# A new order of all groups in a planned attention-and-mixer kernel on one core

## The chip, the core and the metric

The kernel runs on one core of a Trainium2 chip. Its engines are TensorE (PE, matmuls; PEld is its weight load), VectorE (DVE), ScalarE (ACT), GpSimd (POOL) and SyncE (SP, which only issues DMAs here). The metric is device time in microseconds (us), less is better. The time before is the median of 13 runs.

## What is computed

A gated linear recurrence over 768 steps (4 batches, 8 heads of 48), and on its output a low-rank mixing over the sequence and a two-layer network over the channels. Inputs and output are float32.

```python
def _attn_ref(q, k, v, alpha):              # all (4, 8, 768, 48)
    for t in range(S):
        state = alpha[:, :, t, :, None] * state + einsum('bhd,bhe->bhde', k[:, :, t], v[:, :, t])
        y[:, :, t] = einsum('bhd,bhde->bhe', q[:, :, t], state)

def _moe_ref(x, U, V, w_ch1, w_ch2):        # x: y as (4, 768, 384); U (768, 32), V (32, 768)
    h = x.transpose(0, 2, 1) @ U @ V
    u = x + h.transpose(0, 2, 1)
    return u + np.maximum(u @ w_ch1, 0.0) @ w_ch2    # 384 -> 1536 -> 384
```

## The kernel before

**Tiling.** The recurrence is worked in units of 128 rows, six to a batch. In batches 0 and 1 a unit is a half of the heads over 256 steps, each partition holding two neighbouring steps (`stage_pair`); in batches 2 and 3 it is all heads over 128 steps (`stage_gla`). "Unit 1.3" is the unit 3 of batch 1. A unit goes through these groups of instructions:

- four loads by SP (alpha, k, q, v) into one of 36 `io` slots;
- ACT takes the logarithm of alpha, PE adds it up by matmuls with triangular masks (the decay sums, L461 to L470 or L685 to L687), ACT forms the exponentials `ai` and `aa` and the decay of the whole unit;
- DVE or POOL scales k and q by them (`rk`, `rq`; L492 or L722), PE transposes both (L507 or L743), ACT or DVE copies the transposed tiles out of PSUM (`kt`, `qt`);
- PE forms the scores (L531 or L759) into two PSUM banks, DVE masks them (`pm`, L542 or L769);
- PE forms the unit's contribution to the state (L570 or L782). In batch 0 a matmul with the identity (L560) adds the state so far on PE, and DVE multiplies the sum by the decay (`st`); elsewhere DVE adds (`sm`), and DVE or POOL multiplies;
- PE forms the output from masked scores and v (`rv`, a bf16 copy) and from q and the state (L617 and L629, or L851 and L849), ACT or DVE copies it to `xb`.

In batch 3 all transpositions of k and q go by DMA instead: ACT issues two `DMA_TRANSPOSE` for each unit (L732 to L736), twelve in all.

`stage_mix` then makes the low-rank sums (L869), the mixed rows and their transposition `uT` (L888 and L891 in batch 0; L903, DVE additions, and L926 elsewhere). `mlp1` makes the hidden layer: 24 groups to a batch, each three matmuls of 384 columns (L953) and a ReLU by ACT or DVE (L963, L965). `mlp2` makes each of six output row blocks in groups of four matmuls (L983), DVE adds the residual (L995), SP stores. The weights come as 24 loads, each copied to bf16 by POOL, ACT or DVE. Mode tags of the groups (F, Q, R, C, V) say how a group tiles the PE array: whole, in quarters, in halves of the rows, in strips of the columns, or in strips of the rows.

**The order.** Every group is handed to a planner with `P.add`, which names the engines that can do it, a cost for each and what it reads and writes; `add` numbers the groups, 0 to 1061. `TABLE` is one list of all the numbers, and the groups are emitted in its order: each engine works off its own groups of that list, in that order, and waits for what they read. A letter behind a number picks the engine (V for DVE, A for ACT, G for POOL); without one the first engine named is taken. `place` walks the list with the planner's own costs, and from that comes two things only: which slot of a ring (PSUM bank, `io` slot and so on) a buffer gets, and how many matmuls on a zero tile ("fillers", L331) go into PE's expected gaps before 28 us. For a DMA that ACT issues it assumes this landing:

```python
if op.mode == "X":
    clock[eng] = t + cost
    end[op] = t + (5000.0 if dma > t + 800.0 else 3800.0) - self.LAT[eng]
    dma = max(dma, t) + 300.0
```

The numbers that the next sections use:

| group | number |
|---|---|
| loads of alpha of 0.1 and 0.4, of q of 0.1 | 71, 83, 73 |
| decay sums of units 0.2, 0.0, 0.1, 0.3, 0.4 | 211, 165, 188, 236, 261 |
| unit 0.0: scaled k; copies of the transposed k and q; scores; masks; contribution and state; identity matmul | 169; 173, 174; 175; 176, 177; 178, 179; 180 |
| unit 0.2: copies of k and q; scores; masks; identity matmuls | 219, 220; 221; 222, 223; 225, 227 |
| unit 0.1: state, identity matmul | 202, 203 |
| hidden-layer groups of batch 0: the first of the old table, the first of the new one; another, with the last of its weight loads and the copy of that | 340, 328; 358, 25, 26 |
| unit 1.0: transposition of k, its copy, scores | 418, 420, 422 |
| unit 1.3: decay sums, scaling of q, its transposition | 483, 488, 490 |
| transposes by ACT: units 3.0 to 3.5 | 871, 872; 888, 889; 906, 907; 924, 925; 942, 943; 959, 960 (k first) |
| scores of units 3.1, 3.4, 3.5 | 890, 944, 961 |
| unit 3.2's scaling of q, its load | 905, 149 |
| ReLUs of batch 0; a ReLU of batch 2 (of hidden-layer group 795); a weight copy of the second layer | 341, 349, 361, 371; 796; 48 |

Of the kernel before, what the change touches and what calls it, by code (L numbers as in the profile page):

```python
# [156 lines left out]


TABLE = """
75 2 3 4 5 209 211 67 76 163 165 79 234 214 167 69 77 68 170V 212 215G 236 217 172 238 213 216V 166 169V 218 171 174V 220V 173V 175 176 83 70 81 237  # L160
168 219A 71 78 164G 80 178 221 179 223 73 72 87 74 0 241G 180 222 181 84 186 259 239 188 210G 240G 190 189 261 224 225 226 177 264 263 192V 1 193G 187G
242 227 243 244A 262 245V 229 230 231 194 246 232V 282 191 196A 233V 228 247 248 182 195 284 197A 184A 201 198 183 85 287 285 265G 82 88 202 266V 267
203 269A 235G 89 268 199 204 200 86 270A 185A 286 249 250 251 271 90 91 7 288G 254 289V 8 260G 95 6 33 99 252 256 35 31 23 39 10 290 258A 253 272 273
292A 19 41 21 37 27 25 107 29 291 255 205 274 275 293A 276 294 257A 295 296 283A 277 57 297 298 279 206 9G 410 34G 32G 412 278 299 208A 207V 300 301
302 304V 101 92 100 47 96 97 94 415 280A 281A 303A 13 16 305 306 93 43 55 45 49 14A 311 308 314 317 307A 51 63 59 53 456 315 309 433 98 103 312 17V
313A 458 318 320 310V 323 321 324 322V 325V 435 11 20V 319V 36A 316A 340 338 342 362 339V 61 436 461 438 341A 366 22G 42G 364 24A 460 363A 12A 38V 40V
365V 352 328 437 367A 414 30A 459 65 102 111 108 104 109 105 329V 343V 26V 28V 463V 106 462G 326 348 349A 506 413 330 368 354 360 355V 331V 336 508
353V 416V 439V 112 346 332 511 347A 369A 333A 372 373V 334 335V 337V 327V 440G 358 356 465 344 464 467V 510 361A 509 359A 442 411G 417G 115 113 444V
345A 357A 466A 418 441 350 419 425 443V 420V 421V 351A 46A 48A 468 15 44G 56G 50G 110 114 426 469 445 422 370 116 424 423 446 470 371A 52A 380 386 54G
64G 429 430 432V 447 58A 431A 434A 374 375 448 452 62G 427 428V 449 60V 66V 450 387 381 453 454A 117 481 483 376 457V 455V 476 471 477 382 486 485 529  # L170
484 531 377 472 512G 514 388 473V 487V 513V 474 516V 515 392 489 488V 451G 383 532 533 517A 491V 479V 389 482G 490 478 492A 480A 535G 534 653 393 496
497 493 518 498G 536G 495 494 119 394 655 537 398 538 379 378 123 390 127 399 499 520 395 519 475G 500G 530G 507A 539A 656 659V 501 521 544 540A 658
657 541 660G 503 661 545 400 502 662A 505A 522 504A 663 542 543 524 547 523G 546V 664V 526 672 549 551A 548 525 550A 674 118 391 124 121 120 129 131
528V 135 133 122 125 527V 665 552 404 676 677 553A 675 692 712 554 654G 401 666 137 139 667 132 126 564 559 555 560 556 561 405 406 557 670 562 668 565
566 694 714 567 563V 669 558A 587 585 589 696 716 695 715 717 590A 732 671V 679V 568V 573 609 605 407 610V 698G 579 615 606V 616V 571 580A 586A 588A
752 591 734 592A 697 700 577 678V 572V 701V 754 673G 719G 699G 756 737 755 680 607 134 613 608V 578V 595 575 682 687 574V 681V 688 614V 611 576A 736
612A 596A 603 702 581 601 703V 689G 597 569 599 604A 582A 735 598A 570A 863 600A 602A 683V 128 385 136 384 408 758G 739G 693G 738G 704 684 705 685 686
583 707 617 740 722 584A 708 723V 718G 865 618 690 867 130 141 403 706 159 151 147 138 757G 709V 691V 866 741A 713G 619 710 761 762A 720 742 593 759
760A 594A 721V 629 620 143 409 146 396 621 622 402 868 727 743V 630 728 140 148 145 155 724 744 898 952 916 753A 733G 18 870G 729G 763 711V 765 726 764
635 636 745 725 746 631 623 747 637 900 901 624 730 750 748 749V 766 767V 632 880 731A 882 902 751A 883 903 885 884 872 625 869G 638 626 768 628 871  # L180
641 642 152 153 627 149 397 142 769V 780 775 776 770 777 771 781 782 643 918 919 772 887G 904G 647 954 648 778 783 649 773 889 920 779V 784V 144 634
150 811 922G 923G 934 956 955 812A 921 924 774V 829 813 873 787 830V 814V 160 874 799 800V 875 650 819 793 815 794V 644 816V 936 809 827 825 810V 823
791 828V 785 905G 881G 864G 886G 899G 788A 925 907 876 906 888 957G 824V 826V 786V 877 797 803 893 821 878 157 792A 798A 938 894 804V 156 154 161 805
806V 801 158 941V 802V 937 879A 939 822A 820A 817 926 890 908 940G 818A 928 959 789 790A 892 891 909 917G 895G 958G 853 910 795 796V 943 942 807 808V
896 831 911 912 833 854 935G 960 914 947 929 927 913V 930 931V 948 949V 915A 832A 858 834 835 859 633 162 855 953V 836 837 944 946 961 945 860 838 839
950 932 652 963 962 646 964 651 645 856 843 840 861 951V 933A 965A 897A 966 848 967A 841 978 968 973 980 975 974 979 844 849 970 969 845 976 977A 857
842 862 981 850 971 982V 1015 1016V 1025 1007 1011 1013 1027 972V 991 1008V 993 994A 1028A 1026A 851 846 1009 995 1001 999 1023 1002A 1014A 1024A 992A
1021 1019 1029 1022V 1012V 1017 1010A 1020A 1018A 983 1046 1047 1030V 1048 1049 984A 989 990V 987 1051 1005 1003 1004V 639 1050 985 1052 997 1053 986V
988V 1054 640 1055 852 996A 1031 1041 1036 998V 1042 1006A 1000A 1043 1044 1032 1037 1038 1033 1056 1045 847 1039 1040 1034 1057 1059 1060 1035 1058
1061  # L190
"""

# [6 lines left out]
def kernel(  # L199
# [12 lines left out]
    nc = tc.nc  # L212
    B, H, S, D = q.shape
    C = 128
    NC = S // C
    HP = H // 2
    DM = H * D
# [23 lines left out]
    P = Plan()  # L241
# [16 lines left out]
    for x in (filler, tri, ident, mask2, blocks):  # L258
        nc.vector.memset(x, 0.0)  # L259
    nc.gpsimd.affine_select(  # L260
        out=tri, in_=tri, compare_op=ALU.is_gt, fill=1.0, base=0, pattern=[[1, 2], [-1, C]], channel_multiplier=1
# [3 lines left out]
        out=mask2, in_=mask2, compare_op=ALU.is_gt, fill=1.0, base=0, pattern=[[1, 2], [-1, 2], [-2, C]], channel_multiplier=2  # L265
# [703 lines left out]
    def mlp2(b, xb, ub, utx, h1, c):  # L969
        tt = c // NT  # L970
        low = b in XT
        base = xb if low else ub
        ou = Buf(outs)
        parts = [(0, 256), (256, DM)] if b == B - 1 and c == NC - 1 else [(0, DM)]
        for n, (lo, hi) in enumerate(parts):
            hb = Buf(bank)
            groups = [range(NJ)] if len(parts) > 1 else [range(4 * g, 4 * g + 4) for g in range(3)]
            for g, jts in enumerate(groups):
                last = jts[-1] == NJ - 1

                def f(e, jts=jts, hb=hb, lo=lo, hi=hi, last=last):
                    for jt in jts:
                        nc.tensor.matmul(  # L983
                            hb()[:, 0 : hi - lo], lhsT=h1()[:, jt, c * C : (c + 1) * C], rhs=w2_sb[:, jt, lo:hi],
                            start=(jt == 0), stop=(jt == NJ - 1 and not low),
                        )
                    if low and last:
                        nc.tensor.matmul(hb()[:, 0 : hi - lo], lhsT=vp_sb[:, c * C : (c + 1) * C], rhs=utx()[:, lo:hi], start=False, stop=True)

                need = [(h1, tt, jt) for jt in jts] + [("w2", jt) for jt in jts] + ([utx] if low and last else [])  # L990
                cost = mm(*[hi - lo] * (len(jts) + (1 if low and last else 0)))
                P.add({"PE": cost}, f, r=need, w=[hb])

            def f_o(e, hb=hb, lo=lo, hi=hi):
                nc.vector.tensor_tensor(ou()[:, lo:hi], base()[:, c, lo:hi], hb()[:, 0 : hi - lo], op=ALU.add)  # L995

            P.add({"DVE": 70 + 398 * (hi - lo) // DM}, f_o, r=[hb] + (xk(b, xb, c) if low else [(ub, c)]), w=[(ou, n)])

            if b not in PAIR:
                P.add(  # L1000
                    {"SP": 550.0 * (hi - lo) / DM + (0 if len(parts) == 1 else 60)},
                    lambda e, lo=lo, hi=hi: nc.sync.dma_start(out[b, c * C : (c + 1) * C, lo:hi], ou()[:, lo:hi]),
                    r=[(ou, n)],
                )
                continue
            for z in range(2):

                def f_store(e, z=z):
                    nc.sync.dma_start(out[b, c * C : (c + 1) * C, :].rearrange("(m j) x -> j m x", j=2)[z], ou()[64 * z : 64 * z + 64, :])

                P.add({"SP": 300.0}, f_store, r=[(ou, n)])

    small()
    weights1()
# [49 lines left out]
```

## Time and profile before

| | |
|---|---|
| median of 13 runs | 163.08 us (161.56 to 164.98) |
| the profiled execution | 161.81 us, its span 160.0 us |
| PE idle before its first matmul | 1.19 us |
| fillers on PE | 16 |
| DMA, bytes moved | 30.39 MB, mean 190 GB/s |
| transposes by ACT: issue to landing, least, median, most | 3.4, 4.5, 6.1 us |
| ACT held by one such issue | 1.21 to 1.67 us |

The span goes from the first to the last instruction on the core; the time has some 1.8 us more around it. The profile gives each engine's busy time, 40 equal slices of the span as tenths of busy time, the share of the core's 16 DMA engines in use, and the chain of waits that ended last. A matmul counts as busy from its issue to its modelled end, and matmuls overlap, so PE shows as busy also where it is held up for less than a matmul's latency of 0.2 to 0.33 us.

### The profile page before, as it was taken

How to read it: one execution, taken by the hardware profiler on the slowest of the kernel's cores; microseconds unless marked ns; L12 is line 12 of the kernel's file. 1: busy time of each engine (PE TensorE's matmuls, PEld its weight loads, DVE VectorE, ACT ScalarE, POOL GpSimd, SP SyncE). 2: the span in 40 equal slices, each digit the busy share in tenths (PEclk: the TensorE clock that was granted, in tenths of full speed). 3: DMA queues.
4: the chain of work that ended last, by engine and by line, in shares of the span. 5: the costliest groups of instructions: out<-in, count | busy, mean ns of one | idle time of the engine just before them, and what ended most of it. 6: DMA issues, size and time to landing. Idle time of an engine off the chain costs nothing.

```text
span 160.0 us, 4734 instructions
## 1 busy us (share of the span) xinstructions
PE 153.3 (96%) x1821; PEld 99.4 (62%) x1821; DVE 119.4 (75%) x275; ACT 84.9 (53%) x224; POOL 53.2 (33%) x85
## 2 busy tenths in 40 slices
PE   6979899999999999999999999999999999999992
PEld 2447677666756667666667665666575656665661
DVE  6189995878897999986777877799998877135341
ACT  6566879978854667578876472613610311572000
POOL 5165742217433374026595206462530000000000
PEclk9999999999999999999999999999999999999999
DMA  5999999999998989999987989999992530002233
GB/s 127 286 300 265 241 223 297 334 318 291 281 325 214 243 171 192 194 211 185 207 189 140 222 172 195 212 200 196 218 170 67 160 117 10 0 0 77 99 118 128
DMA packets 89910, 30.39 MB, mean 190 GB/s; under 512 B 83584, under 2 KB 89856, under 8 KB 89888
## 3 DMA queue, kind: packets, MB, share of 16 engines
q1 hardware_dynamic: 83360, 28.52, 72.8%
q10 hardware_dynamic: 6528, 1.57, 8.0%
q8 instruction: 14, 0.23, 0.6%
q14 instruction: 8, 0.07, 0.1%
HBM read 23.79 MB, written 4.72 MB: 178 GB/s over the span
## 4 chain that ended last, share of the span: by engine, by line
PE 79%; DMA 9%; SPq 5%; DVE 3%; issue 2%; ACT 0%; DVEq 0%
PE ps L983 29%; PE ps L953 25%; SPq L411 5%; DMA io<-in_alpha_dram 4%; DMA io<-in_v_dram 3%; DMA kt<-rk 3%; PE ps L507 2%; PE ps L759 2%; PE ps L926 2%; PE ps L743 2%; PE ps L617 2%; PE ps L531 2%; PE ps L570 1%; PE ps L869 1%; PE ps L851 1%
## 5 line engine op out<-in xcount | busy, mean ns | idle before, releaser
L983 PE MATMUL ps<-w_sb,h1t 128*128 128x384 bf16 (+2 forms) x300 | 53.5, 320 | 0.0
L953 PE MATMUL ps<-uT,w_sb 128*128 128x384 bf16 x288 | 50.9, 326 | 0.0
L953 PEld LDWEIGHTS <-w_sb 128*128 128x128 bf16 x288 | 27.0, 98 | 16.3
L983 PEld LDWEIGHTS <-h1t 128*128 128x128 bf16 x300 | 26.7, 98 | 16.2 <-issue 1.9
L963 ACT ACTIVATE h1t<-ps 128x384 bf16<-128x384 f32 x52 | 23.7, 499 | 19.7 <-PE ps L953 19.1
L965 DVE TENSOR_SCALAR h1t<-ps 128x384 bf16<-128x384 f32 x44 | 22.7, 551 | 10.5 <-PE ps L953 9.4
L769 DVE TENSOR_TENSOR pm<-ps,maskc 128x512 bf16<-128x512 f32 x24 | 15.1, 682 | 2.9 <-PE ps L759 2.9
L995 DVE TENSOR_TENSOR ou<-ub,ps 128x384 f32<-128x384 bf16 (+2 forms) x19 | 9.8, 528 | 8.7 <-PE ps L983 7.8
L542 DVE TENSOR_TENSOR pm<-ps,maskp 128x512 bf16<-128x512 f32 x24 | 15.5, 681 | 0.5 <-PE ps L531 0.5
L722 POOL TENSOR_TENSOR rk<-io,ai 128x384 bf16<-128x384 f32 x10 | 9.2, 926 | 17.2 <-PE ps L869 7.1
L338 ACT CAST xb<-ps 128x192 bf16<-128x192 f32 (+1 forms) x22 | 7.7, 377 | 12.7 <-PE ps L851 6.1
L342 POOL CAST rv<-io 128x384 bf16<-128x384 f32 x18 | 9.3, 521 | 12.7 <-DMA io<-in_v_dram 9.7
L492 POOL TENSOR_TENSOR rk<-io,ai 128x384 bf16<-128x384 f32 x7 | 6.5, 928 | 12.2 <-ACT ai L477 4.4
L911 DVE TENSOR_TENSOR ub<-xb,ps 128x384 bf16<-128x384 bf16 x18 | 8.6, 548 | 2.2 <-PE ps L903 2.2
L722 POOL TENSOR_TENSOR rq<-io,aa 128x384 bf16<-128x384 f32 x10 | 9.4, 946 | 2.7 <-DMA io<-in_q_dram 1.1
L695 ACT ACTIVATE ai<-ps 128x384 bf16<-128x384 f32 x12 | 5.8, 498 | 5.7 <-PE ps L687 5.7
L441 ACT ACTIVATE lt<-io 128x384 bf16<-128x384 f32 x12 | 6.1, 523 | 4.2 <-DMA io<-in_alpha_dram 4.1
L342 POOL CAST w_sb<-io 128x384 bf16<-128x384 f32 x10 | 5.1, 531 | 8.4 <-DMA io<-in_moe_w_ch_dram 8.4
L492 DVE TENSOR_TENSOR rq<-io,aa 128x384 bf16<-128x384 f32 x7 | 4.8, 692 | 3.9 <-ACT aa L478 3.7
L338 ACT COPY kt<-ps 128x512 bf16<-128x512 bf16 x10 | 5.9, 587 | 2.8 <-PE ps L743 1.3
L331 PE MATMUL ps<-filler 128*128 128x512 bf16 x16 | 6.2, 493 | 1.2 <-DVE filler L259 1.2
L696 ACT ACTIVATE aa<-ps 128x384 bf16<-128x384 f32 x12 | 5.8, 496 | 2.4 <-POOL rk L722 1.1
(133 smaller groups left out, 243.5 us busy)
## 6 DMA issues: line engine op xcount, KB each, us to landing
io<-in_alpha_dram SPq DMA_DIRECT2D x24, 192.0 KB, 3.9
io<-in_k_dram SPq DMA_DIRECT2D x24, 192.0 KB, 4.0
io<-in_q_dram SPq DMA_DIRECT2D x24, 192.0 KB, 3.9
io<-in_v_dram SPq DMA_DIRECT2D x24, 192.0 KB, 3.9
io<-in_moe_w_ch_dram SPq DMA_DIRECT2D x24, 192.0 KB, 4.4
out_dram<-ou SPq DMA_DIRECT2D x24, 96.0 KB, 2.9
out_dram<-ou SPq DMA_DIRECT2D x11, 192.0 KB, 1.9
out_dram<-ou SPq DMA_DIRECT2D x1, 128.0 KB, 1.7
```

The lines of the kernel that those rows point to most:

```text
L338: nc.scalar.copy(dst, src)
L342: nc.gpsimd.tensor_copy(dst, src)
L492: eng.tensor_tensor(jh(dst()[:, :, 0:D]), raw(a), jh(x()), op=ALU.mult)
L542: nc.vector.tensor_tensor(dst, s2, maskp.to_broadcast([C, 2, 2, C]), op=ALU.mult)
L722: eng.tensor_tensor(dst()[:, :, 0:D], a(), x(), op=ALU.mult)
L769: nc.vector.tensor_tensor(pm()[:, :, par, :], s2, maskc.to_broadcast([C, HP, C]), op=ALU.mult)
L911: P.add({"DVE": 465}, lambda e, c=c, hb=hb: nc.vector.tensor_tensor(ub()[:, c, :], xb()[:, c, :], hb()[:, 0:DM], op=ALU.add), r=[hb] + xk( ...
L953: nc.tensor.matmul(hb()[:, 0:TW], lhsT=w1_sb[:, ct, jt * 128 : (jt + 1) * 128], rhs=uT()[:, ct, tt * TW : (tt + 1) * TW], start=(ct == 0), ...
L963: nc.scalar.activation(dst, hb()[:, 0:TW], AF.Relu)
L965: nc.vector.tensor_scalar_max(dst, hb()[:, 0:TW], 0.0)
L983: nc.tensor.matmul(hb()[:, 0 : hi - lo], lhsT=h1()[:, jt, c * C : (c + 1) * C], rhs=w2_sb[:, jt, lo:hi], start=(jt == 0), stop=(jt == NJ - ...
L995: nc.vector.tensor_tensor(ou()[:, lo:hi], base()[:, c, lo:hi], hb()[:, 0 : hi - lo], op=ALU.add)
```

## The change

`TABLE` is replaced as a whole by another order of the same 1062 groups. The engines that groups are given to change too: ACT gets 222 groups (before 217), POOL 73 (78), DVE 244 as before, PE 363, SP 160. Of the 96 ReLUs 25 go from ACT to DVE and 18 from DVE to ACT. The store of batches 0 and 1 is written with its column bounds, which are 0 and 384 in these batches. No constant of the planner is touched.

```diff
 TABLE = """
-75 2 3 4 5 209 211 67 76 163 165 79 234 214 167 69 77 68 170V 212 215G 236 217 172 238 213 216V 166 169V 218 171 174V 220V 173V 175 176 83 70 81 237
-168 219A 71 78 164G 80 178 221 179 223 73 72 87 74 0 241G 180 222 181 84 186 259 239 188 210G 240G 190 189 261 224 225 226 177 264 263 192V 1 193G 187G
-242 227 243 244A 262 245V 229 230 231 194 246 232V 282 191 196A 233V 228 247 248 182 195 284 197A 184A 201 198 183 85 287 285 265G 82 88 202 266V 267
-203 269A 235G 89 268 199 204 200 86 270A 185A 286 249 250 251 271 90 91 7 288G 254 289V 8 260G 95 6 33 99 252 256 35 31 23 39 10 290 258A 253 272 273
...
-313A 458 318 320 310V 323 321 324 322V 325V 435 11 20V 319V 36A 316A 340 338 342 362 339V 61 436 461 438 341A 366 22G 42G 364 24A 460 363A 12A 38V 40V
-365V 352 328 437 367A 414 30A 459 65 102 111 108 104 109 105 329V 343V 26V 28V 463V 106 462G 326 348 349A 506 413 330 368 354 360 355V 331V 336 508
-353V 416V 439V 112 346 332 511 347A 369A 333A 372 373V 334 335V 337V 327V 440G 358 356 465 344 464 467V 510 361A 509 359A 442 411G 417G 115 113 444V
-345A 357A 466A 418 441 350 419 425 443V 420V 421V 351A 46A 48A 468 15 44G 56G 50G 110 114 426 469 445 422 370 116 424 423 446 470 371A 52A 380 386 54G
...
-150 811 922G 923G 934 956 955 812A 921 924 774V 829 813 873 787 830V 814V 160 874 799 800V 875 650 819 793 815 794V 644 816V 936 809 827 825 810V 823
-791 828V 785 905G 881G 864G 886G 899G 788A 925 907 876 906 888 957G 824V 826V 786V 877 797 803 893 821 878 157 792A 798A 938 894 804V 156 154 161 805
-806V 801 158 941V 802V 937 879A 939 822A 820A 817 926 890 908 940G 818A 928 959 789 790A 892 891 909 917G 895G 958G 853 910 795 796V 943 942 807 808V
-896 831 911 912 833 854 935G 960 914 947 929 927 913V 930 931V 948 949V 915A 832A 858 834 835 859 633 162 855 953V 836 837 944 946 961 945 860 838 839
...
+75 67 71 79 209 163 211 186 188 165 234 77 76 68 236 70 69 80 166 191 168 81 78 213 212 72 83 169V 171 238 167 216V 215V 218 217 239 189 220A 214 170V
+173A 164A 190 237 241G 240G 4 219V 221 222 172 223 174V 178 243 179 74 192V 1 180 242 175 187G 181 73 177 87 82 85 176 245A 210A 224 259 261 225 226
+244A 193G 262 264 263 201 246 194 202 203 247 227 195 282 197A 196A 228 204 248 235G 2 3 84 182 183 184A 284 249 250 198 266V 185V 251 286 287 285 88
+268 254 255 265G 89 270A 256 267 252 200 199 229 230 231 269A 253 86 90 91 288G 8 7 6 257A 232A 289V 290 19 99 271 292V 260G 10 5 291 272 273 258A 233A
+293A 205 207A 274 275 206 95 23 21 27 283A 208A 410 29 33 35 25 31 107 294 24G 20G 276 296 39 295 22G 93 96 101 41 277 279 281A 278 297 298 299 9A 280A
+37 94 47 412 300 92 97 43 11 301 302 304V 303V 314 100 49 45 103 28G 30G 98 55 53 57 51 102 59 61 109 63 16 13 415 12A 456 413 17V 305 306 433 14A 65
+317 320 458 307V 321 308 309 311 460 322A 105 108 104 318 315 316V 111 312 310A 313A 323 319A 324 435 438 461 328 330 326 459 36A 414 436 325V 34V 26V
+32G 350 358 332 334 329V 506 437 40A 327A 356 336 359A 337A 351V 335V 106 362 508 340 331A 354 357V 333V 463G 342 352 465 364 510 42A 363V 355V 439V
+509 511 441 443A 353A 365A 38G 366 360 113 112 411V 417V 467V 367V 115 343A 372 419 416G 338 425 370 421A 341A 361A 48A 371A 440V 44G 418 348 344 442
+462G 426 427 339V 349A 420A 345A 373V 428V 444V 464 50G 54G 58G 466V 368 422 468 445 423 369V 446 447 469 424 52G 481 483 46A 380 346 374 386 434A 484
+486 56A 347A 485 448 449 450 60G 457V 513G 451G 114 110 62A 64A 387 429 452 453 375 430 381 116 117 66A 119 431V 470 454V 432V 455V 476 471 515 517V
+382 392 477 388 472 473V 479V 474 383 0 488G 487G 389 512V 478 376 490 480A 529 531 534 532 489 514 475V 492V 482V 516V 377 393 496 535G 518 491A 493
...
+864G 779V 774V 160 150 809 821 801 827 954 923G 802V 810V 828V 822V 956 883 886G 823 797 805 791 650 824A 876 813 806A 792A 925 887V 789 873 877 814V
+790V 905G 888 907 889 156 157 161 154 875 874 893 811 793 794V 785 798V 786V 815 819 787 831 955 936 816V 812V 788V 820V 799 825 803 829 158 894 937
+939 938 832A 800V 826V 830A 804V 817 926 899G 818A 895G 928 957G 959 940V 908 890 942 892 927 891 878 858 795 859 853 807 796A 911 896 941G 958G 879V
+910 943 917G 935G 854 929 960 912 833 947 909 913V 834 930 932 855 931G 808V 948 646 645 897A 162 856 835 944 945 961 953A 857 652 651 639 640 633 838
...
             for z in range(2):
 
-                def f_store(e, z=z):
-                    nc.sync.dma_start(out[b, c * C : (c + 1) * C, :].rearrange("(m j) x -> j m x", j=2)[z], ou()[64 * z : 64 * z + 64, :])
-
-                P.add({"SP": 300.0}, f_store, r=[(ou, n)])
+                def f_store(e, z=z, lo=lo, hi=hi):
+                    nc.sync.dma_start(out[b, c * C : (c + 1) * C, lo:hi].rearrange("(m j) x -> j m x", j=2)[z], ou()[64 * z : 64 * z + 64, lo:hi])
+
+                P.add({"SP": 20 + 280.0 * (hi - lo) / DM}, f_store, r=[(ou, n)])
```

## The prediction

> **What bounds the kernel now.** I read the page first, then the busy time by stretch, the waits of TensorE (PE), its timeline, and the chain that ended last. All times are microseconds.
>
> ```profile
> span 160.0 us, 4734 instructions
> PE 153.3 (96%) x1821; PEld 99.4 (62%) x1821; DVE 119.4 (75%) x275; ACT 84.9 (53%) x224; POOL 53.2 (33%) x85
> PE   6979899999999999999999999999999999999992
> ```
>
> PE is busy 96% of the span, and its gaps stand in the first six slices and the last one. VectorE (DVE) at 75% is the next. The stretches put numbers on it:
>
> ```profile
> core 0: us, PE busy (x) PEld busy (x) DVE busy (x) ACT busy (x) POOL busy (x), PEclk, DMA share, GB/s
> 3.94:28.59 24.65, 22.74 (x421) 15.82 (x420) 17.71 (x44) 18.05 (x50) 10.61 (x17) 1.00 1.01 271
> 28.59:157.00 128.41, 127.86 (x1399) 82.66 (x1395) 98.90 (x205) 64.45 (x170) 40.54 (x57) 1.00 0.80 179
> 157.00:160.00 3.00, 0.00 (x0) 0.00 (x0) 0.29 (x1) 0.00 (x0) 0.00 (x0) 0.95 0.21 67
> ```
>
> 3.94 is the first matmul of a decay group, 28.59 the first hidden-layer matmul (L953). Between them the DMA share is 1.01: the opening waits for data. From 28.59 to 157.00 PE idles 0.55 in all. After 157.00 come one addition and the last stores, the same groups in both tables.
>
> ```profile
> PE ps L507 <- DVE rq L492: 0.3, 1, 0.3
> PE ps L759 <- DMA kt<-rk: 0.2, 1, 0.2
> ```
>
> These are all of PE's waits after 29 (waiter, line, releaser: total, times, longest). They understate, as a matmul's latency counts as busy. So I took every PE group's distance to the next one's start and subtracted what its matmuls take in the trace when nothing is late: start to start 0.162 for 384 columns (45 in 7.31 on the chain), 0.056 for 128, 0.042 for 96, 0.025 for 48 and less. What is left over, mode changes (below) taken out, is 7.4 from 3.94 to 28.59, and 0.98 after it: 0.51 at the transposition of q of unit 1.3 (L507, 53.4) and 0.36 at the scores of unit 3.1 (L759, 113.2), the rest crumbs.
>
> Changing the tiling mode between groups costs PE time too:
>
> ```profile
> 43.23 1.46 PE L983 MATMUL ps<-w_sb,h1t 128*128 128x384 bf16 x8
> 44.63 0.37 PE L617 MATMUL ps<-rv,pm 64*128 64x48 bf16 x16
> ```
>
> Eight matmuls need 1.30, the next group, of 64 rows, starts after 1.40: 0.096 for a change, and the same extra at the others.
>
> **The change, part by part.** It reorders; no group is added or removed, and the store's slice is the whole row wherever that function runs (batches 0 and 1 have one part, 0 to 384). So PE's work is the same 137.5 (the sum of such distances over its 363 groups). What can differ is mode changes, fillers, and waits.
>
> *Mode changes*, counted along the two tables: 69 before (29 up to the first L953 group, 40 behind), 75 after (34 and 41). Behind the opening: +1 x 0.096 = **+0.1**. The five in the opening, 0.48, can hide in its waits.
>
> *The opening.* The same 74 PE groups stand ahead of the first L953 group in both. The first 24 loads are the same, permuted, so I give each the landing that its place had in the trace: alpha of unit 0.1 goes from 10.48 to 5.14, alpha of 0.4 from 8.71 to 12.63, q of 0.1 from 12.63 to 15.69. Following the new order by rows: k of 0.0 lands at 8.06, its scaling on DVE takes 0.56, its transposition starts at 8.8; q of 0.2 is copied by ACT (0.59), k of 0.2 by DVE (0.42), so the first scores (221) start at 10.85, before 10.39. DVE then has two masks (0.60 apart), the copy 174 and the state 179 (0.35) ahead of identity matmul 180: it starts at 13.3, before 11.85. Three fillers (0.21 each, 17 after against 16) fall into that wait. At 14.4 the new order lacks the decay sums 261 (0.45) and identity matmuls 225 and 227 (0.18) that the old one has done: 0.65 behind. From there the old one still waits 2.25 before 28.59. The new one, by the same rows, waits 0.45 for state 202 and some 0.2 at each of four score groups, about 1.3, and pays 0.3 of the extra mode changes: 0.65 + 0.3 - 0.95 = 0.0, at best. If none of the waiting is won back it is 0.65 + 0.48 = +1.1. A floor speaks against a gain: the fifth L953 group (358) now needs the 38th load, whose place landed at 30.12; with the copy on DVE (0.36) and 0.15 to be seen it starts at 30.63 at the earliest, four groups (1.95) after the first, which so starts no sooner in effect than 28.68, +0.1. Bounds +0.1 and +1.1; I take **+0.4**, nearer the floor, because the steps end there.
>
> *Waits behind the opening.* (a) DVE's 0.51: PE groups worth 10.0 now stand between the decay sums of unit 1.3 (483) and that transposition (490), before 5.3, and q's scaling (488), POOL's job now, has the room; so -0.5, at worst 0 is saved. (b) ACT copies k of 1.0 (420) behind four ReLUs and a weight copy (341, 361, 48, 371, 349), 0.4 apart: 5 x 0.4 + 0.59 + 0.15 to be seen = 2.75, where PE has 2.3 of work between transposition 418 and scores 422: +0.45, at best 0; I take +0.4. Behind that copy ACT's next ReLU waits and its PSUM bank with it. (c) The transposes that ACT issues, for units 3.0 to 3.5:
>
> ```profile
> 109.21 4.48 DMA kt<-rk
> ...
> 115.05 1.39 ACTq L734 DMA_TRANSPOSE qt<-rq  x1
> 116.55 1.21 ACTq L734 DMA_TRANSPOSE kt<-rk  x1
> 117.88 1.21 ACTq L734 DMA_TRANSPOSE qt<-rq  x1
> ...
> DMA to landing us min/median/max: 3.4/4.5/6.1
> ```
>
> In the first line (the chain) the scores of 3.1 wait for the landing at 113.69. Each issue holds ACT 1.2 to 1.7. In the new order 3.3 q, 3.1 k, 3.2 q, 3.1 q are issued in a row; q of 3.2 is the 131st DMA of SP, whose place landed at 105.8, POOL scales it in 0.93, and 3.1 q follows 1.3 later than 3.2 q: with the two ahead, at some 109.5. Landing after the median 4.5, at 114.0; its scores are due at 113.6 plus what the opening loses. Wait 0 to 0.4 there, but 1.6 at a landing of 6.1 and none at 3.4. What stands behind on ACT, the exponentials of 3.5 and 3.4, moves with it, and ReLU 796 now stands ahead of the last two transposes: 3.5 q issues at 118.3 to 118.9 (before 117.88) and lands at 122.5 to 123.5, scores 961 being due at 122.8 plus 0.5: 0 to 0.5. Together 0.6 against 0.36 before: +0.2; bounds -0.4 and +1.7. Sum of (a) to (c): **+0.1**, bounds -0.9 and +2.2.
>
> Here the Trainium skill speaks, page "DMA: Bandwidth & Descriptors", section "Issuing engines are not separate DMA queues": DMAs of ScalarE and SyncE end on the same 16 DMA engines and interleave, and issuing elsewhere saves only the sequencer's time, which it calls usually small beside the DMA. The first half says that no order gives these transposes a lane of their own, which is against this change; the second the rows deny, 1.2 to 1.7 of 4.5 being over a quarter. By the page's small issue, 3.1 q would go out about 3 sooner, (c) would be -0.4 and the sum of the change 0.0; by the rows it is as above.
>
> *Sum.* 0.4 + 0.1 + 0.1 = +0.6. The profiled execution took 161.81 (160.0 and 1.81 around it), so 162.4 like for like; the median of the 13 runs stands 1.27 above it, so 163.08 + 0.6 = **163.7**.
>
> **Rivals.** *The waits really go* (faster): the opening at its floor, (a) and the old transposition wait gone, (b) hidden: 0.1 + 0.1 - 0.98 = -0.8. The median run loses 1.27 more than the profiled one; if half of that is such waits, -1.4: **161.7**. For it: the new table leaves more PE work between most producers and users in the opening. Against it: the floor, and +0.4 on ACT. *Transposes land late* (slower): 3.1 q lands after 6.1, scores 890 wait 1.5, 961 0.5: 0.4 + 0.1 + 0.4 - 0.5 + 1.5 + 0.5 - 0.36 = +2.0, **165.1**; it decides once a landing is over 4.6 behind its issue. For it: 6.1 was measured at 115.05, beside the v load of 114.94. Against it: the other landings were mostly 4 to 5. *The opening is not made up*: 1.1 + 0.1 + 0.1 = +1.3, **164.4**. *The change doesn't do what it says*: the planner's two landing costs are untouched, so only the order carries the assumption; that alone is 0, inside the forecast.
>
> **How the numbers follow.** Forecast 0.45 (its own range 162.9 to 164.4), faster rival 0.25, late transposes 0.20, opening 0.10. A measurement here tells no change from about 0.5%, 0.8. Faster is the one rival: 0.25. Of the forecast 0.30 lies within 0.8 of 163.08. Slower: 0.15 + 0.20 + 0.10 = 0.45. The range leaves a tenth on either side: 161.6 (the faster rival) to 165.4 (a little over the late transposes).
>
> **What would show it.** The first L953 matmul at 28.7 to 29.6; identity matmul 180 (the first L560) near 13.3; DVE's wait at L507 near 53 gone; a wait of L531 near 42 (scores 422) behind ACT; L759 near 114 and 123 waiting for a transposed tile by up to half a us. I am wrong if the first L953 starts before 28.4, if L759 waits over 1, or if PE stands still anywhere else for over 0.3.

## The result, and the profile after

| | before | after |
|---|---|---|
| median | 162.89 us (161.56 to 165.38, 48 runs) | 164.09 us (163.15 to 165.39, 11 runs) |
| ratio | | 1.0091, interval 1.0064 to 1.0117 |
| profiled execution, its span | 161.81 us, 160.0 us | 165.05 us, 163.0 us |

The new order is slower: by 0.9% in the ratio, by 1.2 us or 0.7% between the medians. (The ratio leaves out executions that are more than 1.5% above the fastest of their kernel, 8 of the 48 before and none after.) The two profiled executions lie 3.2 apart, because the one of before is 1.1 below its median and the one of after 1.0 above its own; a difference of those two traces alone shows more than there is, so each was taken a second time (below).

The busy times of the changed kernel, the 40 slices of PE, and the same three stretches as before (to the first L953, to the last matmul, behind it):

```profile
span 163.0 us, 4733 instructions
PE 155.4 (95%) x1822; PEld 100.1 (61%) x1822; DVE 122.3 (75%) x275; ACT 87.3 (54%) x229; POOL 50.6 (31%) x80
PE   6799999899999999999999999999799999999992
```

```profile
core 0: us, PE busy (x) PEld busy (x) DVE busy (x) ACT busy (x) POOL busy (x), PEclk, DMA share, GB/s
4.04:30.51 26.47, 24.24 (x422) 16.36 (x421) 17.77 (x39) 20.56 (x58) 10.29 (x19) 1.00 0.94 249
30.51:160.00 129.49, 128.45 (x1400) 82.89 (x1397) 101.66 (x205) 64.36 (x168) 38.87 (x55) 1.00 0.78 178
160.00:163.00 3.00, 0.00 (x0) 0.00 (x0) 0.29 (x1) 0.00 (x0) 0.00 (x0) 1.00 0.21 69
```

The first hidden-layer matmul starts 1.92 later than before (30.51 against 28.59), the stretch behind it is 1.1 longer (129.49 against 128.41), the tail is the same 3.00. Behind the first hidden-layer matmul the slices have one new dent, the 7 near 116; ahead of it the eighth slice went from 9 to 8. The waits of PE from 26 to 160 (waiter, line, releaser: total, times, longest) are three:

```profile
PE ps L759 <- DMA qt<-rq: 0.9, 1, 0.9
PE ps L891 <- ACT vp_sb L338: 0.7, 1, 0.7
PE ps L953 <- DVE uT L340: 0.2, 1, 0.2
```

The chain that ended last holds the first two of them (start, duration, what):

```profile
22.80 5.11 DMA io<-in_alpha_dram
...
27.99 0.07 ACT lt L441
28.06 0.36 issue
28.42 0.47 ACT vp_sb L338
28.89 0.04 issue
28.93 0.32 PE ps L891
...
112.84 4.78 DMA qt<-rq
117.61 0.14 issue
117.75 0.40 PE ps L759 x8
```

*The opening.* ACT's queue has the copy of `vp_sb` (group 14, which the mixed rows of L891 read) behind the logarithm of unit 1.1 (433), which has nothing to do with them. Its alpha was issued at 22.80 and landed at 27.91, 5.11 later; the load issued just before it had landed at 24.99. So ACT stands, and PE with it.

*The transposes.* q of unit 3.1, issued at 112.84, lands at 117.61, 4.78 behind its issue, and its scores wait, 0.14 more being the way from landing to matmul.

*The third wait* is DVE's: its queue has an output addition of batch 1 ahead of the copies of `uT` that the first hidden-layer group of batch 2 reads, and that addition waits for the store of an earlier block to leave its buffer (in brackets how long DVE was idle, and for what):

```profile
102.56 0.55 DVE L995 TENSOR_TENSOR ou<-ub,ps 128x384 f32<-128x384 bf16 x1 [0.46 <-DMA out_dram<-ou]
103.04 1.48 DVE L340 COPY uT<-ps 128x768 bf16<-128x768 bf16 x3
```

Measured as in the prediction (distances between PE groups less their streaming and less 0.096 for each mode change), and with a second execution of each, with times of 161.70 for the old order and 164.45 for the new:

| trace | span | first L953 | waiting before it | waiting behind it | scores of 3.1 and 3.2 | `uT`, batch 2 | q of 1.3 | mode changes |
|---|---|---|---|---|---|---|---|---|
| old | 160.0 | 28.59 | 7.40 | 1.36 | 0.36 | 0 | 0.51 | 69 |
| old again | 159.9 | 28.38 | 7.16 | 1.43 | 0.94 | 0 | 0 | 69 |
| new | 163.0 | 30.51 | 8.74 | 2.36 | 1.04 | 0.32 | 0 | 75 |
| new again | 162.5 | 29.52 | 7.77 | 2.85 | 1.01 | 0.27 | 0 | 75 |

Both traces of the new order differ from both of the old one in the same ways: the hidden layer starts 0.9 to 2.1 later, and the stretch behind its start waits 0.9 to 1.5 more, first of all at the scores and at `uT`. (For the first row's 1.36 the prediction has 0.98. Its two waits of over 0.3, 0.51 and 0.36, are the same in both; the rest is remainders of under 0.1.)

### The profile page after: what moved, and what is told of

Its sections match the earlier page's. It is cut to its first block, busy times and chain, and to the rows that moved or that the text cites. A ratio compares the mean times of both kernels' runs of the same rounds, so it can differ in the third digit from the quotient of the medians.

```text
span 163.0 us, 4733 instructions
## 1 busy us (share of the span) xinstructions
PE 155.4 (95%) x1822; PEld 100.1 (61%) x1822; DVE 122.3 (75%) x275; ACT 87.3 (54%) x229; POOL 50.6 (31%) x80
## 4 chain that ended last, share of the span: by engine, by line
PE 69%; SPq 13%; DMA 8%; DVE 5%; issue 2%; ACT 1%; DVEq 0%; ACTq 0%
PE ps L983 27%; PE ps L953 23%; SPq L411 10%; DMA io<-in_alpha_dram 3%; DMA qt<-rq 3%; DMA out_dram<-ou 2%; DVE h1t L965 2%; PE ps L507 2%; PE ps L743 2%; PE ps L759 2%; PE ps L851 2%; PE ps L926 1%; SPq L387 1%; PE ps L869 1%; PE ps L531 1%
## 5 line engine op out<-in xcount | busy, mean ns | idle before, releaser
L953 PE MATMUL ps<-uT,w_sb 128*128 128x384 bf16 x288 | 51.1, 326 | 0.2 <-DVE uT L340 0.2
L953 PEld LDWEIGHTS <-w_sb 128*128 128x128 bf16 x288 | 27.1, 98 | 16.7 <-issue 0.4
L965 DVE TENSOR_SCALAR h1t<-ps 128x384 bf16<-128x384 f32 x51 | 25.9, 548 | 10.2 <-PE ps L953 9.9
L963 ACT ACTIVATE h1t<-ps 128x384 bf16<-128x384 f32 x45 | 19.7, 501 | 14.3 <-PE ps L953 11.1
L338 ACT CAST xb<-ps 128x192 bf16<-128x192 f32 (+1 forms) x20 | 7.0, 377 | 13.0 <-PE ps L629 5.2
L722 POOL TENSOR_TENSOR rk<-io,ai 128x384 bf16<-128x384 f32 x9 | 8.3, 923 | 15.0 <-ACT ai L695 9.8
L342 POOL CAST rv<-io 128x384 bf16<-128x384 f32 x13 | 6.4, 504 | 13.2 <-DMA io<-in_v_dram 11.2
L342 POOL CAST w_sb<-io 128x384 bf16<-128x384 f32 x13 | 6.5, 508 | 11.0 <-DMA io<-in_moe_w_ch_dram 10.9
L492 POOL TENSOR_TENSOR rk<-io,ai 128x384 bf16<-128x384 f32 x7 | 6.4, 914 | 8.9 <-ACT ai L477 5.6
L492 POOL TENSOR_TENSOR rq<-io,aa 128x384 bf16<-128x384 f32 x5 | 4.5, 909 | 13.5 <-DMA io<-in_q_dram 10.2
L338 ACT COPY qt<-ps 128x512 bf16<-128x512 bf16 x12 | 7.1, 590 | 2.6 <-PE ps L507 1.4
L722 POOL TENSOR_TENSOR rq<-io,aa 128x384 bf16<-128x384 f32 x8 | 7.6, 954 | 2.3 <-ACT aa L696 1.7
L331 PE MATMUL ps<-filler 128*128 128x512 bf16 x17 | 6.9, 530 | 1.2 <-DVE filler L259 1.2
```

Source lines behind the costliest of these rows:

```text
L338: nc.scalar.copy(dst, src)
L342: nc.gpsimd.tensor_copy(dst, src)
L492: eng.tensor_tensor(jh(dst()[:, :, 0:D]), raw(a), jh(x()), op=ALU.mult)
L722: eng.tensor_tensor(dst()[:, :, 0:D], a(), x(), op=ALU.mult)
L953: nc.tensor.matmul(hb()[:, 0:TW], lhsT=w1_sb[:, ct, jt * 128 : (jt + 1) * 128], rhs=uT()[:, ct, tt * TW : (tt + 1) * TW], start=(ct == 0), ...
L963: nc.scalar.activation(dst, hb()[:, 0:TW], AF.Relu)
```

## The experiments

Every kernel below is an order of the same 1062 groups, so none leaves work out. Ratios are to the kernel before. In the diffs a line is a piece of `TABLE`.

**The same two kernels again.** The changed kernel, unedited:

> The new order unchanged, for a second trace beside the first. Ratio 1.009 again (1.006 to 1.012). Theory 'opening': the hidden layer (first L953) starts 1.0 to 2.0 us later than the 28.59 of before, and PE waits for a copy of vp on ACT that stands behind a logarithm (L441) whose load is late. Theory 'transposes': the waits behind the opening (L759 for a DMA-transposed tile) are 1.0 us again, and the opening's loss in the first trace was an accident of the load stream, so it shrinks to under 0.7.

163.37 against 162.43, ratio 1.0069 (1.003 to 1.0107). The loss is there a second time. The wait at L891 is not: its alpha came in time, and instead the first L953 waited 1.07 for a weight (the 32nd load landed at 28.45, 3.3 behind the 31st). The 1.0 at the scores is there again, this time at those of unit 3.2, whose q landed at 116.78, 0.13 ahead of the matmul, as 0.14 in the first trace. The profile names a mask on DVE that ended at 116.88, but that is the mask of unit 3.3, which these scores don't need; by the slots that `place` gives, both of their banks had been read by 116.01. So it is the landing here too.

> The old order against itself, for a second trace of it. Ratio 1.000, within 0.003. Theory 'transposes and scores': behind the opening PE again loses 0.3 to 0.8 us at the scores of unit 3.1 and 0.5 us at L507 of unit 1.3, and nothing over 0.3 us elsewhere. Theory 'accident of the load stream': the first L953 starts 1 us or more later than the 28.59 of the first trace, so that the two orders' openings are alike.

162.46 against 162.26, ratio 1.0016 (0.9993 to 1.0039): no difference, as it must be. Here the 0.51 at the transposition of q of unit 1.3 is missing, and the scores of 3.1 wait 0.94. What a single trace had shown of the old order's waits was partly that execution's own.

**Half of each order.** The old order up to the point where its opening ends, then the rest in the order of the new one, and the other way about:

```diff
-(old) 20V 319V 36A 316A 340 338 342 ...
+(old) 20V 319V 36A 316A (rest of new) 24G 22G 28G 30G ...

-(new) 324 435 438 461 328 330 326 ...
+(new) 324 435 438 461 (rest of old) 0 34G 32G 325V ...
```

> All groups that the old table lists ahead of its first L953 group in the old order, everything else in the new order. Theory 'opening': ratio 1.000 to 1.003 (what is left is the transposes' wait and one mode change). Theory 'transposes': ratio 1.006 to 1.009, nothing is won back.

> All groups that the new table lists ahead of its first L953 group in the new order, everything else in the old order. Theory 'opening': ratio 1.006 to 1.009. Theory 'transposes': ratio 0.999 to 1.003. If the two halves each give about 1.004, both theories are half right.

166.12, ratio 1.0229 (1.0169 to 1.0289), and 166.81, ratio 1.0249 (1.0181 to 1.0316). Both theories missed: the halves don't add. The timeline of PE in the second one (start, duration, instructions, in brackets what it waited for) shows why:

```profile
28.33 0.24 PE L470 MATMUL ps<-onesel,lt 128*128 128x2 bf16 x4
31.45 0.82 PE L953 MATMUL ps<-uT,w_sb 128*128 128x384 bf16 x4 [2.88 <-POOL w_sb L342]
```

The new opening is done by 28.45 here, as early as the old one, and then its hidden layer lacks a weight for 2.9: each opening lists the weight loads in the order in which its own hidden layer uses them. In the first hybrid the same seam costs 1.49, 1.06 and 0.39 at L953. These two kernels don't say which half loses the time; they say that loads and their users can't be taken from different orders. The scores of 3.1 still wait as in the order that they come from: 1.01 in the first kernel, 0.76 in the second.

**ACT's logarithm moved.** The wait at L891 taken away, by the logarithm of unit 1.1 going behind group 313 on ACT:

```diff
-305 306 433 14A 65
+305 306 14A 65
...
-310A 313A 323 319A
+310A 313A 433 323 319A
```

> The new order with one group moved: the logarithm of unit 1.1 (433) goes on ACT from ahead of the copy of vp (14) to behind the third copy of uT (313). Theory 'opening': PE's wait of L891 for that copy (0.7 to 0.9 in the first trace) is gone, the time falls by 0.5 to 1.0 us, ratio 1.003 to 1.006. Theory 'transposes': the wait was an accident of one execution; ratio 1.009 as the new order itself.

164.33, ratio 1.0137 (1.0088 to 1.0185): no gain. (The traced execution, 163.37, is the fastest of its six, so it doesn't show where the median lost.) The first L953 starts at 29.23 and nothing waits at L891. But PE now waits 0.8 for the decay sums of unit 1.1, which come right behind that logarithm:

```profile
PE ps L759 <- DMA qt<-rq: 0.9, 1, 0.9
PE ps L461 <- ACT lt L441: 0.7, 1, 0.7
```

The late load isn't there this time: the alpha of unit 1.1 landed at 25.25. The logarithm now stands behind three copies of `uT` on ACT and ends at 28.75, so this wait is the edit's own. The run takes the wait at L891 away and puts another in its place; what a late alpha would have cost here it doesn't show.

**More PE work ahead of the scores.** Three PE groups that stood just behind the scores of 3.2 and 3.1 (an output, a second-layer group and a hidden-layer group; some 1.3 of work) go ahead of them:

```diff
-959 940V 908 890
+959 940V 878 858 795 908 890
...
-927 891 878 858 795 859 853
+927 891 859 853
```

> The new order with three PE groups (an output of unit 3.0, one group of the second layer, one of the hidden layer: 878, 858, 795) moved from behind the scores of units 3.2 and 3.1 to ahead of them, 1.5 us of matmuls. Theory 'transposes': the wait of 1.0 us before these scores, which all four runs with the new order behind the opening show, shrinks to under 0.2, ratio 1.001 to 1.004. Rival 'it moves': the transposes behind them come no sooner, so the us turns up at the scores of 3.4 and 3.5, ratio 1.006 to 1.009.

162.76, ratio 1.0036 (1.0005 to 1.0067). PE's waits behind 26 are down to one line:

```profile
PE ps L953 <- DVE uT L340: 0.2, 1, 0.2
```

The wait at L759 is gone and has turned up neither at the scores of 3.4 and 3.5 nor at the outputs behind the masks; the most behind it is 0.20, at a second-layer group near 118 whose bank a mask was still reading. Against the two measurements of the unedited order (1.0091 and 1.0069) that is 0.0033 to 0.0055, 0.5 to 0.9 us. The difference to the first is just clear of the noise, the one to the second isn't: those two intervals overlap from 1.0030 to 1.0067. What is clear is that the wait of 1.0 to 1.4, which the five traces without this edit have, is gone. This is the one edit of the new order that won time.

**The weights earlier.** Two alpha loads of batch 1 put behind the weight load 21, the work that hangs on them moved to just ahead of and behind the first hidden-layer groups, and four later loads of batch 1 (105, 108, 104, 111) a little further back:

```diff
-290 19 99 271 292V
+290 19 271 292V
...
-275 206 95 23 21 27 283A
+275 206 23 21 95 99 27 283A
...
-415 12A 456 413 17V 305 306 433 14A 65 317 320 458 307V 321
+415 12A 413 17V 305 306 14A 65 317 320 307V 321
...
-309 311 460 322A 105 108 104 318 315 316V 111 312 310A
+309 311 322A 318 315 316V 312 310A
...
-323 319A 324 435 438 461 328 330 326 459 36A 414 436 325V 34V
+323 319A 456 433 105 108 104 111 324 328 330 326 458 435 460 438 461 459 436 36A 414 325V 34V
```

> The new order with what units 1.1 and 1.2 need (two alpha loads, two logarithms, two decay sums and what ACT does with them) moved behind the first hidden-layer groups, so that the first weights are two loads earlier in SP's queue. Theory 'opening': the first L953 starts by 28.5, 1 to 2 us earlier than in the two traces of the new order, ratio 1.000 to 1.004. Rival: the later groups wait for their weights anyway (the fifth for the 36th load), so the time stays, ratio 1.006 to 1.009.

164.78, ratio 1.0139 (1.0107 to 1.0172). The first L953 starts at 27.46, earlier than in any other kernel here, and all of it is given back, and more: the stretch behind waits 4.80 instead of 2.4 to 2.9. Of the waits from 26 on, these at the hidden layer are not in the first trace of the new order:

```profile
PE ps L953 <- POOL w_sb L342: 0.6, 1, 0.6
PE ps L953 <- ACT aa L478: 0.5, 1, 0.5
...
PE ps L953 <- ACT ai L477: 0.2, 1, 0.2
```

The hidden layer starts sooner and runs into PSUM banks that aren't free. At 31.35 and 32.52 (0.36 and 0.68 by the distances) it takes banks of decay sums that ACT has only just read, for the exponentials `ai` and `aa` that were pushed back. At 39.73 (0.78) the profile names a copy of a weight by POOL, but that weight is one of the second layer. The three copies that this group reads had ended by 36.01, and its bank held a transposed q that DVE copied until 39.68. The fifth group (358) doesn't wait. So the rival was right that an earlier start of the hidden layer doesn't win the time, but not in its reason (late weights), and the time didn't stay, it grew.

**The store's slot.** The edit of the scores, and two stores of batch 1 put directly behind the addition that fills them, so that the slot which the third wait needs is freed sooner; the same with the weights' edit too:

```diff
-146 626 148 902
+146 626 627 628 148 902
...
-622 155 627 952 153 628 152 142
+622 155 952 153 152 142
```

> Both edits together, and the two stores of block 1 of batch 1 moved right behind the addition that fills them, so that the addition of block 4 of batch 1 (and the copies of uT behind it, for which PE waits 0.3 us near 103) doesn't wait for them. If opening and transposes both carry the loss: ratio 0.993 to 0.999. If the loss only moves: 1.004 to 1.009.

> New order with the edit of the scores (three PE groups moved ahead of the scores of unit 3.1) and, in addition, the two stores of output block 1 of batch 1 put directly behind their addition on SP. Theory: the new order's wait of 0.3 before the first hidden-layer group of batch 2 (copies of uT queued on DVE behind an addition that waits for that store's slot) goes and nothing else moves: 0.3 us less than with the scores alone (1.0036), so a ratio of 1.001 to 1.003. Rival: the earlier store pushes something else back (a load that stands behind it on SP, and through it an exponential on ACT), as the combined edit of before had waits of 0.8 and 1.0 at batch 2's hidden layer: ratio 1.005 to 1.012, with waits of 0.3 or more between 100 and 110.

166.03, ratio 1.0227 (1.0193 to 1.0262), and 165.23, ratio 1.0167 (1.0133 to 1.0201). The `uT` wait is gone in both, and for its 0.3 the second kernel pays some 2.1 (1.0167 against the 1.0036 of the scores' edit alone). SP's queue in the second kernel (start, time held, DMA):

```profile
90.05 0.59 SPq L418 DMA_DIRECT2D io<-in_v_dram  x1
95.97 1.11 SPq L1009 DMA_DIRECT2D out_dram<-ou  x2
97.18 0.80 SPq L418 DMA_DIRECT2D io<-in_k_dram  x1
98.02 0.76 SPq L1009 DMA_DIRECT2D out_dram<-ou  x1
98.83 0.59 SPq L418 DMA_DIRECT2D io<-in_alpha_dram  x1
```

From 90.64 to 95.97 SP issues nothing: it stands at the stores until the addition is done (95.95), and the loads stand behind. With the scores' edit alone, a load of k went out at 90.10 and an alpha at 91.62 in that time; here they go at 97.18 and 98.83. PE pays at 108.91, 106.28 and 110.78, in the order of these lines:

```profile
PE ps L953 <- ACT ai L695: 0.8, 1, 0.8
PE ps L953 <- ACT aa L696: 0.5, 1, 0.5
PE ps L953 <- DVE st L793: 0.4, 1, 0.4
```

In the first two lines it is hidden-layer groups whose banks hold decay sums that ACT reads late. Both kernels are slower than any of their expectations had it. The second one's rival named the way (a load behind the store, through it an exponential), at too low a price.

**The old order with more work ahead of its scores.** Two hidden-layer groups with their ReLUs go ahead of the scores of 3.3, 3.1 and 3.2, and the output of 3.1 (896) goes three groups later. The expectation names groups 789 and 795; the kernel moves 795 and 807, of the same 0.98:

```diff
-820A 817 926 890
+820A 817 795 796V 807 808V 926 890
...
-853 910 795 796V 943 942 807 808V 896 831 911 912 833 854 935G
+853 910 943 942 831 911 912 833 896 854 935G
```

> Old order with the same kind of edit: two hidden-layer groups of batch 2 (789, 795; 0.98 of PE work) moved ahead of the scores of units 3.3, 3.1 and 3.2, and the output of unit 3.1 put three groups later. Theory (the scores of 3.1 wait for a transposed tile in the old order too, 0.36 and 0.94 in its two traces, and more PE work ahead of them covers it): 0.4 to 0.9 us less than before, ratio 0.994 to 0.998, no wait of over 0.2 at L759 near 113. Rival (the wait is only moved: to the scores of 3.4 and 3.5, to the output of unit 3.1 that waits for masks, or to a hidden-layer group whose PSUM bank isn't free): ratio 1.000 to 1.003 with a wait of 0.3 or more between 114 and 124.

161.62 against 162.57, ratio 0.9951 (0.9922 to 0.9979): faster than both kernels, by 0.5%. The ratio is as expected, the trace isn't:

```profile
113.79 0.40 PE L759 MATMUL ps<-qt,kt 48*128 48x128 bf16 x8
114.46 0.62 PE L759 MATMUL ps<-qt,kt 48*128 48x128 bf16 x16 [0.28 <-DMA kt<-rk]
```

The scores of 3.1 still wait, 0.45 by the distances: the tile landed at 114.41, 5.15 behind its issue at 109.26, where the two traces of the old order have 4.48 and 4.63. By the old landing of 113.69 or 113.56 there would have been none; without the edit, at this landing, the wait would have been some 1.4. That fits the theory, but the profiled execution (161.55) is hardly under the old order's (161.81 and 161.70), so the trace doesn't show where the 0.95 of the medians came from; the ReLUs that now stand ahead of the masks on DVE are part of this edit as well. That the kernel is faster is measured, why is only argued.

The same, with the transposition of q of unit 1.3 moved behind a second-layer group, and another such group moved ahead of the contribution of unit 1.3:

```diff
-389 482G 490 478 492A 480A 535G
+389 482G 478 480A 535G
...
-653 393 496 497
+653 393 490 492A 394 496 497
...
-494 119 394 655 537
+494 119 655 537
```

> As the old order with the scores edit, and the transposition of q of unit 1.3 (490) moved behind the next second-layer group (393, 0.65), with group 394 moved ahead of the contribution of unit 1.3. Theory (the 0.51 that PE waited there in the trace of before is in most runs): a further 0.3 to 0.5 less, ratio 0.991 to 0.996. Rival (that wait was of one execution, the second trace of the old order has none): the same ratio as with the scores alone, within 0.15%. Second rival (the later contribution of unit 1.3 delays the state, and L629 or L570 wait near 58 to 60): 0.2 to 0.6 more than with the scores alone.

162.15, ratio 0.9989 (0.9961 to 1.0017): the gain isn't seen again, though the two intervals overlap. Nothing waits at L507 near 53, and nothing did in the trace of the kernel without this edit either; new are 0.54 at an output of batch 2 near 95, 0.51 in the sums of batch 3 near 129 and 0.36 in the scores of unit 3.2 near 115.7, far from the place of the edit. None of the three expectations had the size. Nor was the wait one execution's: of the five traces of kernels that leave group 490 in its old place, three have it (0.51 in the first, 0.46 in the second hybrid and in the kernel of the next experiment) and two don't. In the first it is q's scaling on DVE that comes last, in the other two an output addition on DVE that frees the bank.

**The price of a mode change.** The old order, with groups of quarters or halves parted by a whole-array group that stood next to them: 16 changes more (85 for 69), in eight places (the expectation counts ten). One of the eight:

```diff
-426 469 445 422 370 116 424
+426 469 370 445 422 116 424
```

> Old order with 16 more changes of the PE tiling mode behind the opening (85 in place of 69): groups of quarters or halves that stood side by side are parted by a group of the whole array that stood next to them, in ten places between 41 and 124; no group goes further than 1.3 us of PE work. Theory (a change costs PE 0.096 wherever it stands, and behind the opening nothing hides it): 16 x 0.096 = 1.5 us more, ratio 1.008 to 1.012, and each parted place longer by 0.19. Rival (the 0.096 is the end of a group's own pipeline and overlaps with the next group's start, or PE has slack behind the opening): ratio 1.000 to 1.004. New waits at masks or outputs that stand closer now are looked for in the trace and are no part of the price.

164.85, ratio 1.0145 (1.0113 to 1.0176), 2.3 us. The timelines of PE at that place, first the old order's second execution, then the edited kernel:

```profile
41.73 0.86 PE L531 MATMUL ps<-qt,kt 48*64 48x128 bf16 x48
42.52 0.66 PE L953 MATMUL ps<-uT,w_sb 128*128 128x384 bf16 x3
43.02 0.49 PE L983 MATMUL ps<-w_sb,h1t 128*128 128x384 bf16 x2
```

```profile
41.80 0.42 PE L531 MATMUL ps<-qt,kt 48*64 48x128 bf16 x16
42.15 0.66 PE L953 MATMUL ps<-uT,w_sb 128*128 128x384 bf16 x3
42.74 0.64 PE L531 MATMUL ps<-qt,kt 48*64 48x128 bf16 x32
43.32 1.47 PE L983 MATMUL ps<-w_sb,h1t 128*128 128x384 bf16 x8
```

The same three groups of scores and one of the hidden layer take 43.02 - 41.73 = 1.29 in the one and 43.32 - 41.80 = 1.52 in the other: 0.23 for two changes. Over all 56 changes behind the opening the median of what is left over at a change is 0.105, and 0.096 over the 40 of the old order. In all, 5.83 is left over at the 56 changes and 3.96 at the 40 of the old order's second trace: 1.87 for 16 changes, 0.117 each, of the 2.6 between the two spans (162.5 and 159.9). The other 0.74 is waits at groups without a change, 0.46 of it at q of unit 1.3, which the old order has in some executions too. The theory had 1.5 and a ratio of 1.008 to 1.012: right in kind, low in size, by the price of a change and by those waits. The rival, that a change costs nothing, is out. The Trainium skill, page "TensorEngine Tiling (Array Packing)", section "Key Properties", says that changing the tiling mode drains TensorE. The traces agree that a change costs PE time, 0.096 to 0.117 here; that it is a drain they don't show by themselves.

## Why the prediction came out as it did

It said 163.7, +0.6, and slower as the likeliest sign; measured are 164.09 and, against the larger count of runs, +1.2 (+0.94 the second time). The direction of most steps held, the sum was half of what it should be. That 164.09 came so near to 163.7 is in part luck: more runs of the old order brought its median down by 0.19, and two terms erred by 0.2 and 0.4 in opposite directions. By its own steps:

- **Mode changes, +0.1 behind the opening and 0.48 in it.** The price held. How much of the 0.48 was hidden can't be told from the openings' other losses.
- **The opening, +0.4.** The two unedited new traces have 1.92 and 0.93 more than the old trace of the sum, three edited kernels that keep this opening or all but one group of it start L953 at 29.12, 29.19 and 29.23, the old opening in its five traces at 28.35 to 28.59. So it is some 0.7 where no load comes very late, inside the bounds of 0.1 and 1.1, and more than that in single executions. The step that was too rough gave each load the landing that its place had in one trace. The third load, the alpha of unit 0.1, lands at 5.12 to 6.26 in the five traces of the new opening (5.14 was used), and the identity matmul 180 started at 12.9 to 14.3 for the 13.3 of the text. The floor held: no kernel with the new opening and its own loads' order started L953 before 29.1. No edit here won the 0.7 back in the time, so it is read from traces and not shown by an experiment.
- **(a) The 0.51 at q of 1.3, -0.5.** Gone in every trace of the new order, as predicted, but it was worth less: three of five traces of the old order have it, 0.3 on average.
- **(b) The copy of k of 1.0, +0.4.** It cost nothing. The scores 422 start without a wait; the 0.12 in the first trace is at the next scores, for a copy by DVE. The copy started 1.29 behind the transposition of k (43.03 and 41.74) and ended at 43.61, ahead of the scores at 43.96: of the five ACT groups in front of it two had started before the transposition, which the working had put behind.
- **(c) The transposes, +0.2 from 0.6 of waiting.** This is the term that was mis-sized. The scores of 3.1 and 3.2 waited 1.0 to 1.4 in each of the five traces that left this place alone, where 0 to 0.4 had been taken, and those of 3.5 nothing, where 0 to 0.5 had been allowed. In the first trace the landing was 4.78 behind the issue instead of 4.5, and the issue was at 112.84 instead of 109.5. The opening's 1.92 accounts for more than half of those 3.3, no term of the working for the rest. The scores were due later too, at 116.7 for 113.6. Against 0.36, 0.94, 0.76 and 0.88 in the four traces that left the old place alone it is +0.4, which the lead of more PE work won back in the new order.
- **Not in the sum:** 0.3 for the `uT` copies behind an addition that waits for a store's slot, 0.24 to 0.50 in each of the six traces that have this part of the new order unedited. The prediction looked at waits for landings and engines, not for an `out` slot.

With 0.7 for the opening, 0.1 for the mode change behind it, 0.3 for `uT`, 0.4 for the scores and nothing for (b), less 0.3 for (a), the sum is 1.2. The medians have 1.2 and 0.94.

Of the prediction's own signs for being wrong, two were met in the first trace: a wait of over 1 at L759 (1.04), and PE standing still for over 0.3 elsewhere (0.89 by the distances at L891, 0.32 at `uT`). The first L953 was named for 28.7 to 29.6; it came at 30.51 in that trace and at 29.1 to 29.5 in the others.

Of the rivals, "transposes land late" had the mechanism and too high a price (165.1): the landing came later than 4.6, the point that it names, and cost 1.0 rather than 1.5 and 0.5. "The opening is not made up" is close as well (+0.7 of its +1.1). "The waits really go" was right only of (a). "The change doesn't do what it says" has something in it: the scores wait longer for transposed tiles in the new order than in the old one. Its four transposes ahead of them land 4.9 to 5.4 behind their issue on average in six traces, the old order's four 4.2 to 4.7 in five. But the last of the four, the one that the scores of 3.1 wait for, is no later: 4.3 to 4.9 against 4.5 to 5.2. The window of those issues, between 104 and 112, in the new order, in the old one and in the old one again:

```profile
104.00:112.00 8.00, 7.90 (x60) 4.78 (x60) 6.75 (x14) 2.02 (x5) 3.98 (x5) 1.00 1.32 199
104.00:112.00 8.00, 8.00 (x68) 5.08 (x67) 7.57 (x16) 1.97 (x5) 3.78 (x6) 1.00 1.19 198
104.00:112.00 8.00, 8.00 (x67) 5.04 (x65) 7.42 (x16) 2.19 (x6) 2.95 (x5) 1.00 1.04 183
```

The last three numbers of a line are clock, DMA share and GB/s: a share of 1.32 in the new order (1.32 to 1.34 in four traces of it), 1.19 and 1.04 in the old one. The four transposes go out among the loads of k, q and v for the last units, which themselves take 4.8 to 6.1 to land there. That more of them at once is why the four are slower on average agrees with these numbers. But the old order with more work ahead of its scores has a share of 1.13 there and a landing of 5.15, so the share alone doesn't tell a single landing, and it wasn't tried by itself.

## What to carry to other kernels

A wait removed from an order comes back where the next queue is in order: behind a store that waits for its data on SP, a logarithm that waits for its load on ACT, an addition that waits for a slot on DVE. So an edit is judged by the time of the whole kernel, and a wait of under 1 us by more than one trace, before it is called a cause. Where an order is already tight, giving the waiting instruction more independent work in front of it on the engine that waits was the only kind of edit that paid, in both orders (from 1.0091 and 1.0069 to 1.0036 in the new one, from 1 to 0.9951 in the old one). Both gains are of the size of the spread between repeats, and a further edit on top of the second didn't keep it.

## What the runs showed of the hardware

- The stream of loads pauses, longer in some executions than in others. With the new opening the landings stop for 2.9 (24.99 to 27.91) in one trace, for 3.3 (25.19 to 28.45) in the next, and for 3.4 (24.86 to 28.28) with the edit of the scores, while SP had gone on issuing: the load that landed at 27.91 had gone out 0.47 behind the one that landed at 24.99. In two other traces of this opening the longest stop between 20 and 32 is 1.9 and 1.8, in the five of the old one 1.7 to 2.1. The three long stops fall behind the 30th, the 31st and the 32nd load, so which group waits depends on which load it meets. What makes the pauses stays open.
- In the first trace of the new order a transpose by ACT lands 4.75 to 5.2 behind its issue while loads run (104 to 113), and 2.3 to 3.8 where few are left (117 to 122). The issue holds ACT 1.20 to 1.53 in both. Over all traces here it is 2.3 to 6.8 and 1.20 to 2.11.
